# One block of weights for several matmuls in succession: reordering two loops of a fused attention and gMLP kernel

## The chip, the cores and the metric

The kernel runs on one core of a Trainium2 chip. The metric is the device time of one execution in microseconds (us), the lower the better. Ratios in this document are the mean time of one kernel's runs over the mean time of the other's runs of the same rounds, so they are not quite the ratio of the medians that are quoted. One execution of the kernel before, the first of all, took 2028.22 us; it is left out, from the medians too. Of the engines, PE is the tensor engine, DVE the vector engine (additions), ACT the one that computes gelu, and SP the one whose queue, SPq, issues the transfers.

## The reference, cut to what matters

Two blocks follow each other: attention with a memory (A) and a gated MLP with mixing over tokens (B). The change touches two products of B: `x @ w_in`, first half, and the last one with `w_out`.

```python
# T = 2048 tokens, D = 1024, F = 3584, Fh = 1792; all inputs bf16
h  = x + A(layernorm(x))
def B(x):
    z  = gelu(x @ w_in)                  # [2048, 3584]
    z1 = z[..., :Fh]                     # product 1: changed (z1 loop)
    z2 = layernorm(z[..., Fh:])
    g  = w_sp @ z2 + b_sp[:, None]       # mixes tokens
    return (z1 * g) @ w_out              # product 2: changed (w_out loop)
h2 = h + B(layernorm(h))
```

## The kernel before

The kernel names each operation to a recorder. From the memory that an operation reads and writes, the recorder works out which earlier operations of other engines, and which transfers, must be done first, and puts waits on semaphores ahead of it. Memory is divided into cells for that: 32 bytes of a partition in SBUF, one bank in PSUM, and 1024 bytes in DRAM.

```python
        kind, base = self.space.get(name, ("dram", 0))
        ...
        if kind == "dram":
            rest = dims
            gran = 1024                  # cell of DRAM, in bytes
        else:
            row = dims[0][0]
            off = off % row
            rest = dims[1:]
            gran = GRAN if kind == "sbuf" else 2048
...
        def run(eng, e):                 # one instruction stream for each engine
            for op in self.ops[eng]:
                for o in op.waits:
                    e.wait_ge(o.dma if o.dma is not None else sems[o.eng], o.val)   # line 208
                ins = getattr(e, op.name)(*op.args, **op.kw)                        # line 209
```

A `matmul(out, lhsT, rhs)` becomes two instructions of the tensor engine (PE): a weight load of `lhsT` (128x128 in the changed loops) and a matmul that streams the columns of `rhs` through it. The kernel uses PSUM as 8 banks of 512 fp32 columns; the loops take them in turn. `fin` is an SBUF buffer for a row block of the output.

```python
    def next_bank():
        b = rot["banks"][rot["n"] % len(rot["banks"])]
        rot["n"] += 1
        return b

    def mm8(dst, lhs, rhs, n=8):
        for i in range(n):
            pe.matmul(dst, lhs(i), rhs(i), start=(i == 0), stop=(i == n - 1))
...
    # z1 loop: 14 blocks of 128 output columns (fc), 4 segments of 512 tokens (s)
    for k in range(4, 8):
        lo, w = CH[k][1:]
        for fl in range(w // 128):
            fc = lo // 128 + fl
            for s in range(NSEG):
                b = next_bank()
                mm8(bank(b), lambda i: WIN[k % 3][:, i, fl * 128:(fl + 1) * 128], lambda i: HNT[s][:, i, :])
                act.activation(Z1T[:, fc, s * 512:(s + 1) * 512], bank(b), ACTF.Gelu_apprx_tanh)
                ...
...
    sp.dma_start(WOUT[:], B_w_out.rearrange("(c p) n -> p c n", p=128))
    for tb in range(4):                  # 4 blocks of 512 tokens
        ...                              # 14 x 16 matmuls: w_sp, then bias and gate into YT
        for tcl in range(4):             # w_out loop: 128 tokens each
            tc = 4 * tb + tcl
            fin = FIN[tc % 3]
            sp.dma_start(fin[:], out2d[tc * 128:(tc + 1) * 128, :])          # h, kept in the output
            for lo, w in ((0, 512), (512, 512)) if tc < NTC - 1 else ((0, 512), (512, 256), (768, 256)):
                b = next_bank()
                hs = slice(lo, lo + w)
                mm8(PS[:, b, 0:w], lambda i: YT[:, i, tcl * 128:(tcl + 1) * 128], lambda i: WOUT[:, i, hs], n=14)
                dve.tensor_tensor(fin[:, hs], fin[:, hs], PS[:, b, 0:w], ALU.add)
                sp.dma_start(out2d[tc * 128:(tc + 1) * 128, hs], fin[:, hs])
```

In the z1 loop the block of weights is `WIN[..., i, fl]`, which is the same for the four segments, but the four segments come one after the other, so each of the 8 blocks is loaded four times. In the w_out loop the stationary block is `YT[:, i, tcl]`, loaded once for each half of the output.

The softmax here doesn't subtract the row's maximum and nothing guards it: scores larger than these inputs give would overflow.

## Time and profile before

| | before |
|---|---|
| time, median of 5 runs | 806.99 us |
| span of the profiled execution | 805.2 us |
| PE busy | 796.1 us (99%) |
| weight loads (PEld) | 5407 loads, 384.7 us (48%), overlapping PE |
| last unbroken stretch of matmuls | 303.3 to 802.5 us |
| z1 loop, w_out loop | 448 matmuls; 462 matmuls |

From the page of the kernel before, its table of busy time and its chain of what ended last:

```profile
PE 796.1 (99%) x5407; PEld 384.7 (48%) x5407; DVE 368.7 (46%) x756; ACT 301.8 (37%) x356; POOL 121.5 (15%) x234
...
PE 92%; DVE 5%; ACT 2%; issue 1%; DMA 0%
```

There is one load for each matmul. A PE that is busy 99% of the time may be badly used all the same. The chain in order of time closes with this line (start, duration, engine, what):

```profile
303.34 499.12 PE ps L209 x2430
```

and the timeline of the kernel before has the z1 groups (8 matmuls each; columns: start us, duration us, engine, line, operation, out<-in, count, and in brackets the idle time of the engine before it):

```profile
417.20 1.89 PE L209 MATMUL ps<-hnT_74,win_117 128*128 128x512 bf16 x8
417.40 0.60 ACT L209 ACTIVATE z1T<-ps 128x512 bf16<-128x512 f32 x1 [1.18 <-PE ps L209]
418.72 1.61 PEld L209 LDWEIGHTS ps<-hnT_75,win_117 128*128 128x128 bf16 x8
418.93 1.89 PE L209 MATMUL ps<-hnT_75,win_117 128*128 128x512 bf16 x8
419.13 0.60 ACT L209 ACTIVATE z1T<-ps 128x512 bf16<-128x512 f32 x1 [1.13 <-PE ps L209]
420.44 1.61 PEld L209 LDWEIGHTS ps<-hnT_76,win_117 128*128 128x128 bf16 x8
420.66 1.89 PE L209 MATMUL ps<-hnT_76,win_117 128*128 128x512 bf16 x8
```

From 417.20 to 420.66 are 16 matmuls: 216 ns each, also where the bank and the gelu change. The duration of a group, 1.89 us, is longer than its share, since a matmul's record (379 ns) runs on while the next has begun. The load of the next group begins 0.2 us before its first matmul, so under a running one. The Trainium skill, "TensorE: Matmul & The Clock Gate", section "Wait — 56ns, not 53.3ns?", gives 215.7 ns from start to start for 512 columns when warm, which is 512 columns at 2.4 GHz and 2.5 ns more. This trace agrees.

Does anything drop a load of a block that the array already holds? The first microseconds answer that: the kernel warms PE with matmuls on one identity block, 12 of them in succession. From the timeline of the kernel before, weight loads only:

```profile
1.59 0.13 PEld L209 LDWEIGHTS ps<-etmp,ident 128*128 128x128 bf16 x2 [1.59 <-DVE ident L209]
2.00 0.15 PEld L209 LDWEIGHTS ps<-etmp,ident 128*128 128x128 bf16 x1 [0.27 <-issue]
2.43 0.15 PEld L209 LDWEIGHTS ps<-etmp,ident 128*128 128x128 bf16 x1 [0.28 <-issue]
```

The loads go on like that, one for each matmul.

### The profile page before, as it was taken

How to read it: one execution, taken by the hardware profiler on the slowest of the kernel's cores; microseconds unless marked ns; L12 is line 12 of the kernel's file. 1: busy time of each engine (PE TensorE's matmuls, PEld its weight loads, DVE VectorE, ACT ScalarE, POOL GpSimd, SP SyncE). 2: the span in 40 equal slices, each digit the busy share in tenths (PEclk: the TensorE clock that was granted, in tenths of full speed). 3: DMA queues.
4: the chain of work that ended last, by engine and by line, in shares of the span. 5: the costliest groups of instructions: out<-in, count | busy, mean ns of one | idle time of the engine just before them, and what ended most of it. 6: DMA issues, size and time to landing. Idle time of an engine off the chain costs nothing.

```text
span 805.2 us, 12550 instructions
## 1 busy us (share of the span) xinstructions
PE 796.1 (99%) x5407; PEld 384.7 (48%) x5407; DVE 368.7 (46%) x756; ACT 301.8 (37%) x356; POOL 121.5 (15%) x234
## 2 busy tenths in 40 slices
PE   8999999999999999999999999999999999999998
PEld 4445544455444455455544444444444444444444
DVE  4653688669854585744463000054233324423332
ACT  3898876886778763233333333100000000000000
POOL 2342433233323231100131000000000000000000
PEclk9999999999999999999999999999999999999999
DMA  9782544455414057611115000550270044011002
GB/s 270 183 171 60 92 80 118 83 95 83 97 40 80 28 158 146 149 46 53 53 53 130 2 1 0 189 120 0 79 138 1 27 101 88 1 59 53 1 7 85
DMA packets 125992, 64.79 MB, mean 80 GB/s; under 512 B 94832, under 2 KB 114928, under 8 KB 125936
## 3 DMA queue, kind: packets, MB, share of 16 engines
q1 hardware_dynamic: 125936, 63.99, 34.1%
q8 instruction: 42, 0.69, 0.4%
q14 instruction: 14, 0.11, 0.1%
HBM read 32.51 MB, written 8.39 MB: 51 GB/s over the span
## 4 chain that ended last, share of the span: by engine, by line
PE 92%; DVE 5%; ACT 2%; issue 1%; DMA 0%
PE ps L209 92%; ACT e_105 L209 1%; DVE ta L209 1%; DVE stats_61 L209 0%; DVE stats_62 L209 0%; ACT e_108 L209 0%; DVE rdm L209 0%; DMA xch_92<-in_A_x_dram 0%; DVE hch_85 L209 0%; DVE rd L209 0%; ACT e_109 L209 0%; ACT e_106 L209 0%; DVE pqk_99 L209 0%; ACT e_104 L209 0%; DVE stats_59 L209 0%
## 5 line engine op out<-in xcount | busy, mean ns | idle before, releaser
L209 PE MATMUL ps<-w_out,yT 128*128 128x512 bf16 (+1 forms) x462 | 97.4, 373 | 0.0
L209 PE MATMUL ps<-wspT_121,z_119 128*128 128x512 bf16 x448 | 97.0, 379 | 0.0
L209 PE MATMUL ps<-wspT_122,z_119 128*128 128x512 bf16 x448 | 97.0, 379 | 0.0
L209 PEld LDWEIGHTS ps<-w_out,yT 128*128 128x128 bf16 x462 | 45.2, 98 | 51.7
L209 PEld LDWEIGHTS ps<-wspT_122,z_119 128*128 128x128 bf16 x448 | 43.8, 98 | 52.8
L209 PEld LDWEIGHTS ps<-wspT_121,z_119 128*128 128x128 bf16 x448 | 43.8, 98 | 52.9
L209 DVE TENSOR_TENSOR tmpg_128<-ps,brow_126 128x512 f32<-128x512 f32 x14 | 9.7, 691 | 117.1 <-DMA brow_126<-in_B_b_sp_dram 96.8
L209 ACT ACTIVATE z_119<-ps 128x448 bf16<-128x448 f32 x64 | 34.8, 544 | 75.1 <-PE ps L209 74.9
L209 PE MATMUL ps<-wo,oT 128*128 128x512 bf16 x256 | 58.4, 379 | 0.0
L209 ACT ACTIVATE z1T<-ps 128x512 bf16<-128x512 f32 x56 | 33.4, 597 | 63.3 <-PE ps L209 63.3
L209 DVE BATCH_NORM_STATS2 zst<-z_119 128x6 f32<-128x448 bf16 x64 | 39.1, 620 | 33.2 <-ACT z_119 L209 33.2
L209 PEld LDWEIGHTS ps<-wo,oT 128*128 128x128 bf16 x256 | 24.4, 98 | 27.4 <-issue 0.4
L209 ACT ACTIVATE e_107<-ps 128x2048 bf16<-128x2048 f32 x16 | 30.0, 1874 | 12.7 <-PE ps L209 12.7
L209 ACT ACTIVATE e_108<-ps 128x2048 bf16<-128x2048 f32 x16 | 30.0, 1877 | 10.7 <-PE ps L209 10.7
L209 ACT ACTIVATE e_104<-ps 128x2048 bf16<-128x2048 f32 x16 | 30.0, 1875 | 10.4 <-PE ps L209 10.4
L209 ACT ACTIVATE e_105<-ps 128x2048 bf16<-128x2048 f32 x16 | 30.0, 1877 | 9.8 <-PE ps L209 9.8
L209 PE MATMUL ps<-xnT_78,wk 128*128 128x512 bf16 x128 | 30.4, 380 | 0.0
L209 PE MATMUL ps<-xnT_77,wk 128*128 128x512 bf16 x128 | 30.4, 380 | 0.0
L209 PE MATMUL ps<-xnT_78,wq 128*128 128x512 bf16 x128 | 30.3, 379 | 0.0
L209 PE MATMUL ps<-xnT_77,wq 128*128 128x512 bf16 x128 | 30.2, 379 | 0.0
L209 PE MATMUL ps<-wv,xnT_77 128*128 128x512 bf16 (+1 forms) x160 | 29.9, 337 | 0.2 <-DMA wv<-in_A_wv_dram 0.2
L209 PE MATMUL ps<-wv,xnT_78 128*128 128x512 bf16 x128 | 29.6, 379 | 0.0
(218 smaller groups left out, 1171.6 us busy)
## 6 DMA issues: line engine op xcount, KB each, us to landing
w_out<-in_B_w_out_dram SPq DMA_DIRECT2D x1, 3584.0 KB, 12.7
wo<-in_A_wo_dram SPq DMA_DIRECT2D x1, 2048.0 KB, 9.9
xr_83<-in_A_x_dram SPq DMA_DIRECT2D x8, 256.0 KB, 3.3
xr_84<-in_A_x_dram SPq DMA_DIRECT2D x8, 256.0 KB, 3.9
win_116<-in_B_w_in_dram SPq DMA_DIRECT2D x2, 896.0 KB, 4.9
wk<-in_A_wk_dram SPq DMA_DIRECT2D x1, 1536.0 KB, 10.9
wq<-in_A_wq_dram SPq DMA_DIRECT2D x1, 1536.0 KB, 14.3
out_dram<-hch_85 SPq DMA_DIRECT2D x6, 256.0 KB, 3.0
```

What stands on the lines that cost most here:

```text
L209: ins = getattr(e, op.name)(*op.args, **op.kw)
```

## The change

The intent: use a block of weights for all products that need it before going to the next one. In the z1 loop four banks are opened at once, and each of the 8 blocks serves the four segments. In the w_out loop two banks are opened, and each of the 14 blocks serves both halves of the output, but for the last row block, whose three parts stay one after the other so that their additions and stores can overlap. The matmuls, their sizes and their number are the same.

```diff
--- before.py
+++ after.py
@@ -785,10 +785,13 @@
         lo, w = CH[k][1:]
         for fl in range(w // 128):
             fc = lo // 128 + fl
+            bs = [next_bank() for _ in range(NSEG)]
+            for i in range(8):
+                for s in range(NSEG):
+                    pe.matmul(bank(bs[s]), WIN[k % 3][:, i, fl * 128:(fl + 1) * 128], HNT[s][:, i, :],
+                              start=(i == 0), stop=(i == 7))
             for s in range(NSEG):
-                b = next_bank()
-                mm8(bank(b), lambda i: WIN[k % 3][:, i, fl * 128:(fl + 1) * 128], lambda i: HNT[s][:, i, :])
-                act.activation(Z1T[:, fc, s * 512:(s + 1) * 512], bank(b), ACTF.Gelu_apprx_tanh)
+                act.activation(Z1T[:, fc, s * 512:(s + 1) * 512], bank(bs[s]), ACTF.Gelu_apprx_tanh)
                 if zq:
                     z2_apply()
         if k + 3 < 8:
@@ -812,10 +815,16 @@
             tc = 4 * tb + tcl
             fin = FIN[tc % 3]
             sp.dma_start(fin[:], out2d[tc * 128:(tc + 1) * 128, :])
-            for lo, w in ((0, 512), (512, 512)) if tc < NTC - 1 else ((0, 512), (512, 256), (768, 256)):
-                b = next_bank()
+            parts = ((0, 512), (512, 512)) if tc < NTC - 1 else ((0, 512), (512, 256), (768, 256))
+            bs = {lo: next_bank() for lo, w in parts}
+            for grp in (parts,) if tc < NTC - 1 else [(q,) for q in parts]:
+                for i in range(14):
+                    for lo, w in grp:
+                        pe.matmul(PS[:, bs[lo], 0:w], YT[:, i, tcl * 128:(tcl + 1) * 128], WOUT[:, i, lo:lo + w],
+                                  start=(i == 0), stop=(i == 13))
+            for lo, w in parts:
+                b = bs[lo]
                 hs = slice(lo, lo + w)
-                mm8(PS[:, b, 0:w], lambda i: YT[:, i, tcl * 128:(tcl + 1) * 128], lambda i: WOUT[:, i, hs], n=14)
                 dve.tensor_tensor(fin[:, hs], fin[:, hs], PS[:, b, 0:w], ALU.add)
                 sp.dma_start(out2d[tc * 128:(tc + 1) * 128, hs], fin[:, hs])
```

## The prediction

> **What bounds the kernel now.** The matrix engine, without a gap, in both places that the change touches. The page gives PE 99% busy of 805.2 us; the chain that ended last closes with one unbroken run of 2430 matmuls, 499.1 us from 303.3 us on, and both changed loops lie in it. The list of waits of the second half has none of PE; the granted clock is 1.00.
>
> The timeline starts the w_in groups (8 matmuls each) at 415.48, 417.20, 418.93, 420.66: 1.726 us, 215.8 ns per matmul. The w_out loop does 112 matmuls from 560.5 to 584.7: 216 ns. The Trainium skill, "TensorE: Matmul & The Clock Gate", section "Wait — 56ns, not 53.3ns?", gives 215.7 ns start to start for 512 columns when warm; this trace agrees. So the columns of the moving operand set the rate. A weight load takes 98 ns (groups by line) and lies under the matmul before it.
>
> **What the change removes, adds, moves.** It is meant to save weight loads: 3 of 4 in the z1 loop (336 of 448), 1 of 2 in w_out for 15 of 16 row blocks (210). I expect none to be dropped: warm-up issues 17 matmuls on one identity block, 12 of them in succession, and the timeline shows 17 loads for them; the page counts 5407 loads for 5407 matmuls. Were all 546 dropped (54 us of load time), each is hidden, so nothing comes off the path. The most that I would allow is the 2.5 ns per matmul above 512/2.4 = 213.3 ns: 546 x 2.5 ns = 1.4 us.
>
> Matmuls, evacuations and transfers keep their number. Moved:
> - z1: four banks close together every 6.9 us instead of one every 1.73 us. ACT has 4 x 0.60 = 2.4 us in a burst; with 8 banks that leaves 4.5 us in hand. No PE wait.
> - The bank switches at each matmul: at today's group borders it switches and the interval stays 215.8 ns. No cost.
> - w_out: both halves close at the end of the block; DVE's two additions (0.69 us each) come back to back. DVE's wait for the fin load (3.2 us before each first half, off the path) goes away, as the first half closes 3 us later.
> - The w_out load starts some 0.7 us later (it overwrites hnT, now read to the end); it takes 13 to 17 us and is needed 48 us later. Free.
> - End: the last block keeps its order. Its fin load is issued about 0.5 us later (today 797.55, landing 800.3); its first additions end near 802.0, before the last one, which waits for PE (802.49).
>
> **On the critical path:** none of it, to within about 1 us.
>
> **Prediction:** 807.0 us, 805.0 to 808.8 at 8 in 10. Faster by over 2%: 0.01; within 2%: 0.98; slower: 0.01.
>
> **What would show it.** Loads still 5407; first gelu of one four to the first of the next 6.90 us; no PE wait after 303 us; DVE's waits on fin loads gone or small; the last addition at about 802.5 us. If loads fall to about 4860 with the time unchanged, the first half of my argument is wrong and the second right.
>
> **What would make it wrong.** A repeated weight load being dropped and that freeing the array between matmuls; a cost for open accumulation in several banks in turn (10 ns per matmul over 868 matmuls would be 9 us); a fin load at the tail that is slow behind two stores (up to 1 us).

## The result, and the profile after

| | before | after |
|---|---|---|
| time, median | 806.99 us (5 runs, 806.83 to 807.07) | 807.40 us (6 runs, 807.30 to 807.53) |
| ratio | | 1.0005, 95% interval 0.9992 to 1.0019 |
| span | 805.2 us | 805.6 us |
| weight loads | 5407, 384.7 us | 5407, 384.6 us |
| last addition starts | 802.49 us | 802.49 us |
| last store is issued | 803.15 us | 803.55 us |

The time is the same within 2%, as predicted. The ranges of the runs do not overlap, though: there is a small loss of about 0.4 us. From the page of the changed kernel:

```profile
PE 790.4 (98%) x5334; PEld 384.6 (48%) x5407; DVE 367.3 (46%) x756; ACT 297.1 (37%) x356; POOL 121.3 (15%) x234
...
PE 91%; DVE 5%; ACT 2%; issue 1%; DMA 0%
```

The loads are all still there. That there are 5334 matmuls and not 5407 is no change of the program: some records are missing from this trace, and their place is left empty, as one sees by the next distance being twice as long. (The kernel before with another cell size, below, has 5334 records too, and two runs of the changed loops, with twice the loads and with the early `fin` load, have 5407.) From the timeline of the changed kernel, z1 loop:

```profile
421.74 0.38 PE L209 MATMUL ps<-hnT_74,win_117 128*128 128x512 bf16 x1
421.74 0.10 PEld L209 LDWEIGHTS ps<-hnT_75,win_117 128*128 128x128 bf16 x1
421.94 2.06 ACT L209 ACTIVATE z1T<-ps 128x512 bf16<-128x512 f32 x4 [5.72 <-PE ps L209]
421.96 0.38 PE L209 MATMUL ps<-hnT_75,win_117 128*128 128x512 bf16 x1
421.96 0.10 PEld L209 LDWEIGHTS ps<-hnT_76,win_117 128*128 128x128 bf16 x1
422.17 0.38 PE L209 MATMUL ps<-hnT_76,win_117 128*128 128x512 bf16 x1
```

The order is the new one (hnT_74, 75, 76 are the segments), the gelus come four at a time, and the distance is 0.216 us still: the next four gelus start at 428.85 us, 6.91 us later, for 32 matmuls. PE's list of waits is empty from 404 us on, before and after. In both traces the first w_out loop starts at 560.52 us, and the `w_sp` matmuls after it at 584.69 us: nothing in these loops has become slower or faster.

What differs is the end. From the timelines, first the kernel before: the additions of the last row block (DVE), and the issue of its stores (SPq, the queue of the transfers).

```profile
800.35 1.03 DVE L209 TENSOR_TENSOR fin_132<-fin_132,ps 128x512 bf16<-128x512 bf16 x2 [3.25 <-DMA fin_132<-out_dram]
801.44 0.43 SPq L209 DMA_DIRECT2D out_dram<-fin_132  x1
802.49 0.42 DVE L209 TENSOR_TENSOR fin_132<-fin_132,ps 128x256 bf16<-128x256 bf16 x1 [1.10 <-PE ps L209]
803.15 0.33 SPq L209 DMA_DIRECT2D out_dram<-fin_132  x1
```

The same lines of the changed kernel:

```profile
800.75 1.02 DVE L209 TENSOR_TENSOR fin_132<-fin_132,ps 128x512 bf16<-128x512 bf16 x2 [3.20 <-DMA fin_132<-out_dram]
801.84 0.43 SPq L209 DMA_DIRECT2D out_dram<-fin_132  x1
802.49 0.42 DVE L209 TENSOR_TENSOR fin_132<-fin_132,ps 128x256 bf16<-128x256 bf16 x1 [0.72 <-PE ps L209]
803.55 0.33 SPq L209 DMA_DIRECT2D out_dram<-fin_132  x1
```

The last addition ends at 802.91 us in both. Yet the last store is issued 0.24 us later in the kernel before and 0.64 us later in the changed one. In both it follows the store of the middle part by 1.71 us. It hangs on that store and not on the addition. The waits of the transfer queue from 800 us on say why (who waited on whom: us in total, times, longest). The kernel before has this one:

```profile
SPq L208 <- DMA out_dram<-fin_132: 1.2, 1, 1.2
```

The changed kernel:

```profile
SPq L209 <- DVE fin_132 L209: 3.4, 1, 3.4
SPq L208 <- DMA out_dram<-fin_132: 1.2, 1, 1.2
```

Line 208 is the wait in the recorder's stream: the queue waits for the landing of a store (1.6 us from issue to landing for these of 64 KB). The output's row has 2048 bytes; the middle part is its bytes 1024 to 1535, the last part 1536 to 2047. In cells of 1024 bytes both lie in one cell, so the recorder takes the last store to overwrite the middle one, and makes it wait.

### The profile page after: what moved, and what is told of

Read it like the earlier page. It is cut to its first block, busy times and chain, and to the rows that moved or that the text cites. A ratio compares the mean times of both kernels' runs of the same rounds, so it can differ in the third digit from the quotient of the medians.

```text
span 805.6 us, 12477 instructions
## 1 busy us (share of the span) xinstructions
PE 790.4 (98%) x5334; PEld 384.6 (48%) x5407; DVE 367.3 (46%) x756; ACT 297.1 (37%) x356; POOL 121.3 (15%) x234
## 4 chain that ended last, share of the span: by engine, by line
PE 91%; DVE 5%; ACT 2%; issue 1%; DMA 0%
PE ps L209 91%; ACT e_105 L209 1%; DVE ta L209 1%; DVE stats_61 L209 0%; DVE stats_62 L209 0%; ACT e_108 L209 0%; DVE rdm L209 0%; DMA xch_92<-in_A_x_dram 0%; DVE hch_85 L209 0%; DVE rd L209 0%; ACT e_109 L209 0%; DVE pqk_99 L209 0%; ACT e_106 L209 0%; ACT e_104 L209 0%; DVE stats_59 L209 0%
## 5 line engine op out<-in xcount | busy, mean ns | idle before, releaser
L209 ACT ACTIVATE z1T<-ps 128x512 bf16<-128x512 f32 x56 | 28.9, 603 | 68.7 <-PE ps L209 68.7
L209 PE MATMUL ps<-xnT_78,wq 128*128 128x512 bf16 x113 | 27.0, 379 | 1.3 <-issue 0.6
L209 PE MATMUL ps<-xnT_77,wq 128*128 128x512 bf16 x113 | 27.0, 379 | 0.9 <-issue 0.2
```

## The experiments

Theory: the moving columns set the rate of PE, and a weight load lies under the matmul before it, so that neither the loads' number nor their order matters; the 0.4 us come from the end of the w_out loop alone. Rivals: (1) the hardware would gain if loads were really saved, and they were not; (2) saved loads gain and the turning through banks takes the gain back; (3) the new order costs a little everywhere.

### Loads really left out

A matmul instruction can be emitted that uses the block which the array holds. The changed kernel, with that for each repeated block:

```diff
+        def held(e, out, lhsT, rhs, start, stop, skip_group_check=False):
+            return e.add_instruction(mybir.InstMatmult(..., ldweights=False, ...))   # same operands, no load
 ...
-                    pe.matmul(bank(bs[s]), WIN[k % 3][:, i, fl * 128:(fl + 1) * 128], HNT[s][:, i, :],
+                    (pe.matmul_held if s else pe.matmul)(bank(bs[s]), WIN[k % 3][:, i, ...], HNT[s][:, i, :],
 ...
-                        pe.matmul(PS[:, bs[lo], 0:w], YT[:, i, tcl * 128:(tcl + 1) * 128], WOUT[:, i, lo:lo + w],
+                        (pe.matmul_held if lo and len(grp) > 1 else pe.matmul)(PS[:, bs[lo], 0:w], YT[...], ...
```

> The changed kernel, with the weight load really left out where the block of weights is the one already held: 336 loads in the w_in loop and 210 in the w_out loop. Theory (columns set the rate, a load lies under the matmul before it): loads fall from 5407 to 4861, the PEld time by about 53 us, the w_in loop stays at 6.90 us for 32 matmuls, and the time stays within 0.3 us of the changed kernel's 807.4. Rival 1 (the 2.5 ns per matmul above 512/2.4 are the load's): about 1.4 us less. Rival 2 (a load takes array time that is hidden in no trace): up to several us less.

Measured: correct, 807.28 us (807.24 to 807.33), ratio to the kernel before 1.0003 (0.9991 to 1.0016). From its page and its timeline:

```profile
PE 790.3 (98%) x5334; PEld 331.3 (41%) x4861; DVE 367.3 (46%) x756; ACT 297.2 (37%) x356; POOL 121.3 (15%) x234
```

```profile
440.33 0.10 PEld L212 LDWEIGHTS ps<-hnT,win 128*128 128x128 bf16 x1 [0.77 <-issue]
440.55 0.38 PE L212 MATMUL ps<-hnT,win 128*128 128x512 bf16 x1
440.76 0.81 PE L219 MATMUL ps<-hnT,win 128*128 128x512 bf16 x3
441.20 0.10 PEld L212 LDWEIGHTS ps<-hnT,win 128*128 128x128 bf16 x1 [0.77 <-issue]
441.41 0.38 PE L212 MATMUL ps<-hnT,win 128*128 128x512 bf16 x1
```

546 loads are gone, 53 us of load time with them, and four matmuls still take 441.41 - 440.55 = 0.86 us, 215 ns each. The time is within 0.12 us of the changed kernel's (in another set of rounds), and the 1.4 us that the prediction allowed at most are not there: the 2.5 ns above 512/2.4 are not the load's. Rival 2 too needs a gain between the changed kernel and this one, which differ in the loads alone. Rivals 1 and 2 fall.

### Twice the loads

The opposite test: a useless load of the same block ahead of each matmul of the z1 loop, 448 more.

```diff
                 for s in range(NSEG):
+                    pe.ldweights_x(bank(bs[s]), WIN[k % 3][:, i, fl * 128:(fl + 1) * 128])   # a bare weight load
                     pe.matmul(bank(bs[s]), WIN[k % 3][:, i, fl * 128:(fl + 1) * 128], HNT[s][:, i, :],
```

> The changed kernel with one useless load more ahead of each of the 448 matmuls of the w_in loop: 896 loads there, 5855 in all. Theory (a load is hidden, with slack: in the narrow pieces of the runs before, matmuls with a load each started 30 ns apart): within 0.3 us of 807.4. Rival (a load needs the array, or there is room for one load ahead only, so the second waits for the running matmul): up to 448 x 30 to 98 ns = 13 to 44 us more.

Measured: correct, 5855 loads, 807.47 us (807.35 to 807.56), ratio 1.0006 (0.9993 to 1.0018). Its timeline has the bare load (L210) and the matmul's own (L212) in pairs:

```profile
440.38 0.10 PEld L210 LDWEIGHTS <-win 128*128 128x128 bf16 x1
440.42 0.10 PEld L212 LDWEIGHTS ps<-hnT,win 128*128 128x128 bf16 x1
440.59 0.10 PEld L210 LDWEIGHTS <-win 128*128 128x128 bf16 x1
```

The time is 0.07 us from the changed kernel's 807.40: two loads under each matmul of 512 columns cost nothing that these rounds can see.

### Each loop alone

The z1 loop changed, w_out as before; and the other way round. The edits undo one half of the diff each.

> Only the w_in loop changed, w_out as before. Theory (the whole 0.4 us comes from the end of w_out): 807.0, as the kernel before; last store issued at 803.15 us as before. Rival (turning through four banks, or gelus in bursts, costs something): part or all of the 0.4 us.

> Only the w_out loop changed. Theory: 807.4, the whole of the difference; the last store is issued 0.4 us later than before although the last addition starts at 802.49 as before. Rival: less than that, the rest in the w_in loop.

Measured in the same rounds: kernel before 806.97 us (806.86 to 807.15); z1 loop alone 806.99 us (806.86 to 807.03); w_out loop alone 807.35 us (807.27 to 807.60). Both correct. The last store of the first is issued at 803.28 us (803.15 was expected; its last addition too starts 0.05 us later than before), of the second at 803.61 us. The whole of the loss is in the w_out loop; rival 3 falls.

### The false dependency of the last store

Cells of 512 bytes in DRAM, in the changed kernel and in the kernel before:

```diff
         if kind == "dram":
             rest = dims
-            gran = 1024
+            gran = 512
```

> The changed kernel, with dependencies in DRAM tracked in units of 512 bytes in place of 1024. The last two stores (256 columns, 512 bytes each of a row) then no longer share a unit, and the last need not wait for the landing of the one before. Theory (the end hangs on that wait: in the changed kernel the last store is issued 0.64 us after its addition has ended, at 803.55): issued right after the addition at about 802.95, 0.5 to 0.6 us off the time, 806.8. Rival (the queue itself spaces the stores, or the end hangs on the addition): no change, 807.4.

> The kernel before with the same finer tracking in DRAM. Theory (its last store also waits for the landing before it, but only 0.24 us past the end of its addition at 802.91): 0.2 us less, 806.8, the same as the changed kernel with finer tracking. Rival (the changed loops cost something of their own): the two differ by the 0.4 us still.

Measured, both correct: changed kernel 806.74 us (806.70 to 806.84) against 806.97 for the kernel before in the same rounds; kernel before with the finer cells 806.86 us (806.73 to 807.01) against 807.04 in its rounds. Each against the kernel before in its own rounds, the changed kernel goes from +0.41 us (807.40 - 806.99) to -0.23 us, the kernel before from 0 to -0.18 us. The two are then 0.05 us apart (0.12 us by their medians), so the changed loops have no cost of their own that these rounds can see. From the timeline of the changed kernel with the finer cells:

```profile
802.47 0.42 DVE L209 TENSOR_TENSOR fin<-fin,ps 128x256 bf16<-128x256 bf16 x1 [0.66 <-PE ps L209]
802.92 0.33 SPq L209 DMA_DIRECT2D out_dram<-fin  x1
```

The store goes out as its addition ends (802.89), and the wait at line 208 is no longer in the list. It is issued 0.63 us earlier than in the changed kernel (803.55), and the time is 0.66 us less, so nothing else that the finer cells may release is needed to explain it. This is the version that is fastest by its median, though by 0.03% of the kernel before, and the interval of its ratio (0.9984 to 1.0009) holds 1.

### The first link of that chain

The changed kernel with its coarse cells, but with the load of the next `fin` issued ahead of this row block's stores:

```diff
-            sp.dma_start(fin[:], out2d[tc * 128:(tc + 1) * 128, :])
+            if tc == 0:
+                sp.dma_start(fin[:], out2d[0:128, :])
 ...
+            if tc < NTC - 1:
+                sp.dma_start(FIN[(tc + 1) % 3][:], out2d[(tc + 1) * 128:(tc + 2) * 128, :])
             for lo, w in parts:
```

> The changed kernel with the fin load of the next row block issued ahead of the stores of this one, and the coarse tracking in DRAM kept. Theory (end: fin load, first additions, store of the middle part, its landing, last store): the first link comes 5 us earlier, so the middle part is stored as soon as its product is there, at about 801.6, lands near 803.2, and the last store goes out near 803.2 in place of 803.55: 807.0 to 807.1. Rival (the fin load does not matter): 807.4.

Measured: correct, 806.87 us (806.76 to 806.92) against 806.98 in the same rounds. The middle store and the last one are issued as the theory had it (801.6 and 803.2):

```profile
801.57 0.33 SPq L209 DMA_DIRECT2D out_dram<-fin  x1
803.17 0.33 SPq L209 DMA_DIRECT2D out_dram<-fin  x1
```

The time came out 0.1 to 0.2 us lower than it said. The wait at line 208 is still there (1.2 us), but it now ends only 0.1 us after the last addition does (803.07). So the chain is: the two additions of row block 14 now come together at its end; the fin load of block 15, which stands behind both of its stores, is issued at 798.01 us in place of 797.55; block 15's first additions start 0.4 us later; its middle store goes out 0.4 us later; and the last store waits for that one's landing.

### Where would a repeated load cost something?

The z1 loop with its 512 columns cut into pieces of 64, once in the order of before, once with each block in succession and its load repeated, once with the repeated load left out. The core of the second edit (the first keeps the order of before inside each piece; the third is the second with `matmul_held` for each repeated block):

```diff
+            for i in range(8):
+                for s in range(NSEG):
+                    for h in range(0, 512, 64):
+                        pe.matmul(PS[:, bs[s], h:h + 64], WIN[...], HNT[s][:, i, h:h + 64],
+                                  start=(i == 0 and h == 0), stop=(i == 7), skip_group_check=True)
```

> The w_in loop in pieces of 64 columns (3584 matmuls in place of 448), order of before within each piece: each matmul has other weights than the one before it. Estimate from the 33-column matmuls of this trace, each with its own load (256 in 14.6 us, 57 ns each): 3584 x 57 ns = 204 us in place of 97, so about 914 us. If loads cost nothing here either: 64/2.4 + 2.5 = 29 ns each, about 815 us.

> The same pieces of 64 columns, 32 matmuls in succession on one block of weights, each still with its load. Theory (nothing drops a repeated load, and here loads set the rate): as the other order, about 914 us. Rival (the engine or the compiler recognises a block that it holds): about 815 us, or fewer loads in the count.

> The same order in pieces of 64 columns, with the repeated loads left out: 112 loads for 3584 matmuls in this loop. Theory (a load is dear only where the matmul is too short to cover it): 29 to 35 ns per matmul, 815 to 840 us, about 80 to 100 us less than with the loads. Rival (short matmuls have a floor of their own near 57 ns): no gain.

Measured, one run each (state unknown, granted clock 1.00), all correct: 820.72, 820.45 and 815.42 us, with 8543, 8543 and 5071 loads. The estimate of 57 ns for a matmul with its own load was wrong. It came from dividing the busy time of a group by its count. Those 33-column matmuls come in fours, and the record of the last one outlasts each four. From the timeline of the kernel before:

```profile
300.48 0.25 PE L209 MATMUL ps<-v,e_104 128*128 128x33 bf16 x4
300.58 0.25 PE L209 MATMUL ps<-v,e_105 128*128 128x33 bf16 x4
300.68 0.25 PE L209 MATMUL ps<-v,e_106 128*128 128x33 bf16 x4
```

Four in 0.10 us are 25 ns each, with another block of weights for each. In the narrow runs the steady distance is likewise the same with and without loads: the first gelu of one four to the first of the next (256 matmuls) is 7.47 us, 29.2 ns each, in both the second and the third (e7 and e8). The 5 us between these runs are stretches in which PE stood still and the profile names no other engine. From the waits of PE in the z1 loop of e7:

```profile
PE ps L209 <- issue: 4.8, 4, 1.8
```

The run without the loads has no such line, and it fetched 53 packets of instructions where the other two fetched 67. By the distances of the gelus, 3.5 us of the 4.8 fall between 431 and 450 us, in which transfers of `w_sp` keep the transfer engines full for long stretches. That PE waited for its own instructions behind these transfers fits, but it was not tested; what is shown is only that 4.8 of the 5 us are four pauses, and not a cost for each load. Leaving loads out did save time here, but by the pauses.

The last run gives each of the 14 column blocks of the z1 loop another form, to find the width at which a load shows:

```diff
+    FORMS = [(512, "other"), (256, "other"), (128, "other"), (128, "drop"), (64, "other"), (64, "same"), (64, "drop"),
+             (32, "other"), (32, "same"), (32, "drop"), (16, "other"), (16, "same"), (16, "drop"), (512, "other")]
```

> The 14 column blocks of the w_in loop in other forms each: pieces of 512, 256, 128, 64, 32 and 16 columns, with another block of weights for each matmul (other), one block in succession with its load repeated (same), and the load left out (drop). Read is the distance from start to start in each. The narrow runs before showed 64 columns at about 29 to 31 ns with and without loads, and a second look at the 33-column matmuls of the kernel before shows 25 ns with a load each. Theory A (loads run beside the matmuls at any of these widths): drop and other alike: about 216, 109, 56, 29, 25, 25 ns, apart from stretches in which the engine waits for instructions. Theory B (a load has a rate of its own that shows below some width): other and same stay above drop at 32 and 16 columns by 10 ns or more.

Measured: correct, 892.06 us (one run, mean granted clock 0.954; this time is compared with nothing). The distances, from the starts of its gelus (a gelu starts when its bank is complete; the 116 in the third line are the matmuls up to the end of the first segment, 7 x 16 + 4):

| columns | another block each time | load left out | how |
|---|---|---|---|
| 512 | 216 ns | | 1.73 us for 8 |
| 256 | 109 ns | | 1.75 us for 16 |
| 128 | 55.8 ns | 55.9 ns | 1.786 us for 32; 6.48 us for 116 |
| 64 | 29.2 ns | 29.2 ns | 1.867 us for 64; 7.47 us for 256 |
| 32 | 25.0 ns | 25.0 ns | 3.20 us for 128; 12.80 us for 512 |
| 16 | 26.9 ns | 25.4 ns | 6.90 us for 256; 26.04 us for 1024 |

The forms with one block and its load repeated gave 29.2 ns at 64 columns, and 28.3 ns at 32 and 28.6 ns at 16 with pauses in them (the list of waits has 0.8 and 1.0 us of them with no engine named, and many short ones escape it). From the gelus of this run, blocks of 32 columns with another block of weights each:

```profile
469.50 0.60 ACT L212 ACTIVATE z1T<-ps 128x512 bf16<-128x512 f32 x1 [1.83 <-PE ps L212]
472.70 0.60 ACT L212 ACTIVATE z1T<-ps 128x512 bf16<-128x512 f32 x1 [2.60 <-PE ps L212]
475.90 0.60 ACT L212 ACTIVATE z1T<-ps 128x512 bf16<-128x512 f32 x1 [2.60 <-PE ps L212]
```

With and without loads the distance is the same at 128, 64 and 32 columns (and at 512, by the run with loads left out), as theory A has it; theory B's 10 ns appear nowhere. The columns do not set the rate at all these widths, though. From 512 and 256 columns one gets (215.8 - 109.2) / 256 = 0.416 ns for a column and 2.6 ns for a matmul, and with that 55.9 ns at 128 and 29.2 ns at 64, as measured to 0.1 ns. At 32 it would be 16 ns, and the runs show 25.0: there something else sets the distance, and it is not the load.

The row of 16 columns was measured at a granted clock of 0.50 (the last section has the stretches). In the first 3.6 us of these matmuls, still at 1.00, they start 25.1 ns apart with a load each. So the 1.5 ns between 26.9 and 25.4 show at the halved clock alone; whether they belong there to the load or to the twice as many instructions is open.

## Why the prediction was right

- **The columns set the rate (right, shown).** 215 to 216 ns per matmul with one load for each, with a quarter of the loads in the z1 loop, and with twice the loads.
- **No load would be dropped (right, shown).** 5407 before and after. Nothing in the program, the compiler or the engine removed a repeated load; it had to be left out by hand.
- **Dropping them would gain nothing, 1.4 us at most (right; the allowance was not needed).** With 546 loads left out, 807.28 us against 807.40.
- **No cost for turning through open banks, none for gelus in fours (right, shown).** The z1 loop alone: 806.99 against 806.97 us.
- **DVE's waits for the fin loads go away (right).** Of 12 such waits in the w_out loops one was left, that of the last row block, which kept its order.
- **An end that does not move (wrong, by 0.4 us).** The prediction had the fin load 0.5 us later (it was 0.46) and the last addition at the same time (it was), and concluded from the last addition to the end. The failed step is the one that took the last addition as what the end hangs on. The end hung on the store of the middle part, through a wait that the recorder's coarse cells made, and that store did move with the fin load. The queue's own list of waits, and the 0.24 us between the end of the addition and the issue of the last store, stood in the profile of before and were not looked at. Among what could make it wrong the prediction named a `fin` load that is slow behind two stores; the load was not slower (2.7 us to landing, 2.8 before), it was issued later. The loss lies within the range that was given. That range, 805.0 to 808.8 us, would have held the 1.4 us gain too: the time alone does not show the mechanism, the experiments do.

## What to carry to other kernels

Before reordering loops to save weight loads, read the distance from start to start of the matmuls: where it is what the columns take, a saved load has nothing to give (here the distance was the same with and without loads at 512, 128 and 64 columns, and also at 32, where it was longer than the columns take; twice the loads were tried at 512 alone). What fewer instructions save in pauses is another matter, as the narrow runs show. Read rates from starts, never from busy time over count, as the record of the last matmul in each burst outlasts it. And follow the end of a kernel to its last transfer, through the waits of the transfer queue: here the only cost and the only gain of the loops at their own width came from a wait for a store that touched other bytes.

## What the Trainium skill lacked or had wrong

- "TensorE: Matmul & The Clock Gate", section "Back-to-back issue gap", gives a sustained roofline for streams of load and matmul of about 131 ns per matmul at 512 columns and about 81 ns at 128. The runs show 216 ns and 55.8 ns, both with a load for each matmul; they agree with the formula that the same section calls the isolated one.
- The same page, Part 3, section "The mechanism", says in its list of what overlaps that a load overlaps matmuls in flight only when its row group differs (the paragraph above that list allows the background buffer as well). All loads of the changed loops fill the whole array, and all are hidden, two of them under one matmul too (807.47 us with 448 more). Part 2, section "Step-by-step: what each phase is for", allows the overlap through a background buffer too; the runs agree that the loads overlap, and do not show by which buffer.
- "Perfetto Trace Analysis", section "Identifying the Most-Contended Engine", recommends, beside the share of peak FLOP/s, the busy share of weight loads as a measure of how near the tensor engine is to its limit. Leaving 546 loads out took that share from 48% to 41% with the time unchanged: it says nothing about the distance to the limit here. The distance between starts does.
- The page on TensorE gives a load's duration by its columns, but no measured figure for how soon one bf16 load can follow another. The runs show records of 98 ns that start closer than that: 40 ns apart with twice the loads, and at 32 columns one load and one matmul every 25.0 ns.
- The same page, section "What's actually happening", has the clock depend on how busy PE has been. In the run of many widths PE had no pause listed above 0.44 us, and yet its granted clock fell from 1.00 to 0.50 3.6 us into the stretch of 16-column matmuls (506.30 to 509.92 us), with no pause listed in between, and came back 3.3 us after the 512-column ones began (588.56 to 591.84 us). From the windows of that run (stretch, us; PE busy and its count; PEld; DVE; ACT; POOL; granted clock; share and GB/s of the transfers):

```profile
500.00:501.00 1.00, 1.00 (x47) 0.00 (x0) 0.00 (x0) 0.00 (x0) 0.00 (x0) 1.00 0.06 16
507.00:508.00 1.00, 1.00 (x46) 1.00 (x43) 0.00 (x0) 0.35 (x1) 0.00 (x0) 1.00 0.00 0
510.00:511.00 1.00, 1.00 (x44) 1.00 (x41) 0.00 (x0) 0.00 (x0) 0.00 (x0) 0.50 0.09 16
575.00:576.00 1.00, 1.00 (x46) 0.11 (x1) 0.00 (x0) 0.00 (x0) 0.00 (x0) 0.50 0.00 0
```

  The first is 32 columns, the second and third are 16 with loads, before and after the fall, the last 16 without loads. No page says that a PE which issues without pause can lose its clock when its matmuls are narrow. It happened once, in one run; at 32 columns the clock stayed at 1.00 for 40 us.
- The same page, Part 2, first step, says that keeping the load apart from the matmul lets one load once and multiply many times. It does not say that this gains nothing where the columns cover the load: 4861 loads in place of 5407 gave the right result in 807.28 us, against 807.40.
